# Rows of means loaded ahead of the fourth input tile, norming by single token tiles, and transposes shifted by a group

## The chip, the cores and the metric

One Trainium2 chip, and one of its cores. The metric is the device time of one launch in microseconds (us), the median of several runs of the same program. Engines are named as the profile names them: PE is TensorE (PEld its weight loads), DVE is VectorE, ACT is ScalarE, POOL is GpSimd, and SP is SyncE, whose queue (SPq) issues nearly all DMAs here.

## The reference

The kernel mixes two branches over the same input of 2048 tokens with 576 features, by a gate per token:

```
x = A_x                                           # [1, 2048, 576]
g = _sigmoid((x * gate_w).sum(-1, keepdims=True))
qkv = (x @ wqkv).reshape(B, S, 3, 32, 18)         # 32 heads of 18
p = softmax(q @ k.T * 18 ** -0.5)                 # per head
a = (p @ v).reshape(B, S, D) @ wo
y = layernorm(x)                                  # over the 576 features, no weights
h = gelu(y @ w1 + b1)                             # 4608 wide
b = h @ w2 + b2
out = g * a + (1 - g) * b
```

## The kernel before

All matrix products split an operand into a rounded high part and the rest, and sum three products of such parts. The program has two parts. The first, some 235 us long, projects the input to queries, keys and values and norms it; the second, some 2,000 us, is one long loop that walks 32 units of attention and fills the gaps of PE with the two products of the mixer branch. The change touches the first part alone.

**The first part** runs over four blocks of 512 tokens (`tb` = 0 to 3), each four token tiles of 128. A block has 17 *groups* (`g` = 0 to 16): nine query/key groups (`qk_group`, lines L881 to L884, 14 matmuls of 512 columns, below q0 to q8) and eight value groups (`v_group`, lines L902 to L905, 14 matmuls of 288 columns, v9 to v16; even and odd halves `n` of the four token tiles). In the blocks 2 and 3 the query/key groups come in the order 4, 0, 1, 2, 3, 5 to 8. Each group takes one of the four accumulator banks of the pool `ps_a`; a query/key group's bank is emptied by a copy on ACT (L887) and a subtraction on DVE (L888), the even value groups' by ACT (L909, L911), the odd ones' by a copy on DVE (L913).

Between the groups of block `tb` stands the work for the next block, at group numbers that the tables `N_AT` and `BLOCK` give:

- `load`: `load_x(tb + 2)` issues two DMAs on SP (L733, 1152 KB, and L736, 128 KB) into one of two buffers for the input.
- `stats`: `norm(.., 0)` and `norm(.., 1)`, in two groups in a row, take mean and variance of the next block on DVE (L844, L845, then a short chain from L850 to L860 with a square root on ACT, L851), and leave them in the tile `stp`.
- `rows`: `stat_rows` turns `stp` with one PE transpose (L826), copies it on ACT (L827), and stores it to DRAM (L828, `st_scr`). `wide`: `load_wide` reads these rows back, spread to all 128 partitions (L832, 512 KB, printed as `qa<-st_scr`). These are the rows of means and of reciprocal deviations, "the means" below.
- `x`: from this group on one `x_chunk` a group for five groups: four PE transposes of 128 columns into one bank (L757, written T0 to T4 below), then on DVE a subtraction that needs the means (L772), a copy on ACT (L774; L778 and L779 in the fifth), and a subtraction on DVE (L775; L780 in the fifth); POOL multiplies by the deviations (L782). The five results are what the next block's groups multiply. `lag` groups later `y_parts` splits the normed chunk (L797 on ACT, L798 on POOL), and one group on `y_store` issues two DMAs (L789, L791).
- `gate`: `norm(.., 2)` and `norm(.., 3)` sum the input times the gate weights on DVE (L867), two token tiles each.

The first block is normed in place instead: `N_AT` says at which group of block 0 which stage runs, and there the stages 2 and 3 also norm the token tile (L870). `y_chunk` (groups 12 to 16 of block 0) transposes the normed tiles again (four transposes, written Y0 to Y4; L805 on ACT, L806 on DVE) and stores them.

In block 1 two *rounds* of attention's first step stand behind the groups 9, 11, 13 and 15 (four matmuls L227 in four banks, each emptied by a DVE reduction L229); they need queries and keys that SP has loaded back (L136). A call of `after(n, f)` runs `f` in `next_turn`, right behind the n-th following group.

Every engine and the SP queue take their instructions in the order in which the code writes them, so a group number moves an instruction on its engine and in every queue that it uses. Which bank a tile of `ps_a` gets follows from that order too. The loop of a block, with its hooks:

```
for g, (fn, args) in enumerate(work):
    ...
    fn(*args)
    next_turn()
    ...
    if tb + 1 < NB:
        at = BLOCK[tb]
        if g == at.get("load"):
            load_x(tb + 2)
        ...
        c = g - at["x"]
        if 0 <= c < 5:
            x_chunk(tb + 1, c)
            after(at["lag"], lambda tb=tb, c=c: y_parts(tb + 1, c))
```

Of the kernel before, what the change touches and what calls it, by code (L numbers as in the profile page):

```python
# [54 lines left out]
          lambda g: 2 * (g in (4, 5, 6, 7, 8, 10, 12, 14))]  # L55
SLOTS = [lambda g: 0, lambda g: 0, lambda g: int(g >= 4), lambda g: 1 if g < 9 else 2]
SKIP = 0
N_AT = {3: 0, 4: 1, 7: 2, 8: 3}
BLOCK = [dict(stats=0, rows=3, wide=4, x=10, lag=4, gate=15, load=16),
         dict(stats=6, rows=9, wide=10, x=12, lag=3, gate=8, load=10),  # L60
         dict(stats=0, rows=3, wide=4, x=6, lag=3, gate=4)]
W_AT = {0: 1, 1: 2, 2: 3, 4: 4, 6: 5, 7: 6}
W_CUT = (0, 128, 416, 704, 992, 2 * D, 3 * D - 288, 3 * D)
NSTEP = 512
# [4 lines left out]
def gated_mix_kernel(ctx: ExitStack, tc: tile.TileContext, x, wqkv, wo, w1, b1, w2, b2, gate_w, out):  # L69
    nc = tc.nc  # L70
    x = x[0]
# [20 lines left out]
    gate = const.tile([P, NT], F32, name="gate")  # L92
# [612 lines left out]
    with ExitStack() as a:  # L705
# [9 lines left out]
        stats = wpool.tile([P, NT, 2], F32, name="stats")  # L715
# [3 lines left out]
        wide = QA[2].bitcast(F32).rearrange("p (a n) -> p a n", a=2)  # L719
# [81 lines left out]
        def y_chunk(tb, c):  # L801
            ps = transposed(tb, c)
            eh = hp.tile([P, TB], F32R, name="hh")
            el = hp.tile([P, TB], F32R, name="hl")
            nc.scalar.activation(eh, ps, AF.Copy)  # L805
            nc.vector.tensor_tensor(el, ps, eh.bitcast(F32), op=ALU.subtract)  # L806
            y_store(tb, c, eh, el)
# [4 lines left out]
        def after(n, fn):  # L812
            queued.append((turn[0] + n, fn))
# [9 lines left out]
        def stat_rows(tb):  # L823

            ps = psum(ps_a)
            nc.tensor.transpose(ps[:, :P], stp, ident)  # L826
            nc.scalar.activation(strow, ps[:8, :P], AF.Copy)  # L827
            nc.sync.dma_start(st_scr[tb], strow)  # L828
# [4 lines left out]

        rstds, junks = {}, {}

        def norm(tb, stage):

            xv = x_view(tb)
            ts_ = slice(4 * tb, 4 * tb + 4)
# [21 lines left out]
            if stage >= 2:  # L861
                if stage == 2:
                    junks[tb] = pp.tile([P, 2, 2, TB], F32, name="p").rearrange("p a b c -> p (a b c)")
                junk = junks[tb]
                for t in (2 * stage - 4, 2 * stage - 3):
                    tt = 4 * tb + t
                    nc.vector.scalar_tensor_tensor(junk[:, :D], xv[:, t, 0:D], 1.0, gwb, op0=ALU.mult, op1=ALU.mult,  # L867
                                                   accum_out=glog[:, tt:tt + 1])
                    if tb == 0:
                        nc.vector.tensor_scalar(xv[:, t, :], xv[:, t, :], stats[:, tt, 0:1], rstds[tb][:, t:t + 1],  # L870
                                                op0=ALU.subtract, op1=ALU.mult)
# [66 lines left out]
        for tb in range(NB):  # L938
            work = [(qk_group, (tb, mt)) for mt in (range(9) if tb < 2 else (4, 0, 1, 2, 3, 5, 6, 7, 8))] + [(v_group, (tb, t, n)) for t in range(4) for n in range(2)]
            for g, (fn, args) in enumerate(work):  # L940
# [12 lines left out]
                next_turn()  # L953
                if tb == 0:
                    if g in N_AT:
                        norm(0, N_AT[g])
                    if g >= 12:
                        y_chunk(0, g - 12)
                if tb + 1 < NB:
# [3 lines that stand above are left out]
                    if g in (at["stats"], at["stats"] + 1):  # L963
                        norm(tb + 1, g - at["stats"])
                    if g == at["rows"]:
                        stat_rows(tb + 1)
                    if g == at["wide"]:
                        load_wide(tb + 1)
                    if g in (at["gate"], at["gate"] + 1):
                        norm(tb + 1, g - at["gate"] + 2)  # L970
                    c = g - at["x"]
                    if 0 <= c < 5:
                        x_chunk(tb + 1, c)
                        after(at["lag"], lambda tb=tb, c=c: y_parts(tb + 1, c))
# [344 lines left out]
```

## Time and profile before

| | before |
|---|---|
| median of 3 runs | 2248.53 us (2248.34 to 2248.68) |
| the profiled execution, its own time | 2250.38 us |
| its span in the trace | 2248.6 us |
| PE busy in the span | 2219.2 us, 99% |
| DVE, ACT, POOL busy | 1643.9, 1426.9, 1003.9 us |
| first part, until the loop begins | about 235 us |

The span runs from the first to the last recorded instruction. PE is busy nearly everywhere, so an edit can only gain where PE stands still or runs at a lower clock, and such places are read from PE's waits and from windows with the granted clock. In the rows of the timeline the first number is the start of a row in us from the start of the span, the second its length; several instructions of a line may be merged into one row (`x12`), and square brackets tell how long the engine was idle before it and what released it.

### The profile page before, as it was taken

The page shows a single profiled execution, that of the slowest core. Times are in us where ns is not written, and L with a number is a line of the kernel's source. Part 1 is how long each engine was busy: PE and PEld are TensorE (multiplying, and loading weights), DVE is VectorE, ACT ScalarE, POOL GpSimd, SP SyncE. Part 2 cuts the span into 40 slices and gives each one's busy share as a digit, 9 for nine tenths or more (in the row PEclk, how much of TensorE's full clock was granted, in tenths as well). Part 3 has the DMA queues.
Part 4 walks back from the last instruction along what each step waited for, and adds up shares of the span by engine and source line. Part 5 has one row for each costly group of instructions (what it writes and reads, how often), then busy time and mean ns, then how long its engine had stood idle before and what let it go on. Part 6 is the DMA issues. An engine that isn't in the chain of part 4 may idle for free.

```text
span 2248.6 us, 51575 instructions
## 1 busy us (share of the span) xinstructions
PE 2219.2 (99%) x20528; PEld 1585.2 (70%) x20528; DVE 1643.9 (73%) x2886; ACT 1426.9 (63%) x2653; POOL 1003.9 (45%) x1001
## 2 busy tenths in 40 slices
PE   8999999999999999999999999999999999999998
PEld 7877766767766777666676767767676676677668
DVE  6576677777777777777777777777776777777734
ACT  3223677777766666666666666666666666666771
POOL 3232666666655444444454444444444444444700
PEclk9999999999999999999999999999999999999999
DMA  7847654444456524333354424233364323242264
GB/s 239 274 155 250 205 177 158 145 157 149 135 199 176 152 101 153 109 114 112 116 145 154 143 95 143 97 121 103 117 178 144 107 99 119 104 145 95 87 221 166
DMA packets 164104, 329.23 MB, mean 146 GB/s; under 512 B 56814, under 2 KB 84074, under 8 KB 153134
## 3 DMA queue, kind: packets, MB, share of 16 engines
q1 hardware_dynamic: 161766, 322.19, 44.3%
q8 instruction: 162, 2.65, 0.5%
q10 hardware_dynamic: 1968, 3.70, 0.4%
q14 instruction: 80, 0.66, 0.1%
q0 software_dynamic: 128, 0.03, 0.0%
HBM read 233.47 MB, written 96.17 MB: 147 GB/s over the span
## 4 chain that ended last, share of the span: by engine, by line
PE 90%; DVE 4%; DMA 2%; ACT 2%; issue 1%; POOL 1%; SPq 0%; ACTq 0%; DVEq 0%; POOLq 0%
PE ps L285 20%; PE ps L572 19%; PE ps L484 19%; PE ps L267 13%; PE ps L227 10%; PE ps L881 3%; PE ps L1204 2%; DVE m L229 2%; PE ps L902 1%; DMA x<-in_B_w_dram 1%; ACT zz L537 0%; POOL w L180 0%; DMA qa<-st_scr 0%; DMA p<-in_A_wqkv_dram 0%; DVE p L772 0%
## 5 line engine op out<-in xcount | busy, mean ns | idle before, releaser
L229 DVE TENSOR_REDUCE m<-ps 128x1 f32<-128x512 f32 x2048 | 1312.3, 685 | 408.2 <-PE ps L227 385.6
L270 ACT ACTIVATE p<-ps 128x512 f32<-128x512 f32 x1368 | 741.2, 596 | 380.6 <-PE ps L267 377.0
L484 PE MATMUL ps<-big,w 64*128 64x512 f32 x3708 | 568.6, 393 | 1.0 <-DVE z L504 0.6
L180 POOL TENSOR_SCALAR zz<-zz 128x512 f32<-128x512 f32 x288 | 178.4, 619 | 749.3 <-ACT zz L537 734.5
L270 ACT ACTIVATE ring<-ps 128x512 f32<-128x512 f32 x680 | 369.1, 596 | 190.2 <-PE ps L267 188.2
L572 PE MATMUL ps<-w,hh 64*128 64x288 f32 x4352 | 483.9, 294 | 1.8 <-DVE x L589 0.9
L267 PE MATMUL ps<-qa,ka 56*128 56x512 f32 x2048 | 459.7, 422 | 3.2 <-ACT p L270 1.8
L572 PEld LDWEIGHTS ps<-w,hh 64*128 64x128 f32 x4352 | 424.0, 186 | 30.1 <-DVE x L589 3.3
L227 PE MATMUL ps<-ka,qa 54*128 54x512 f32 x2048 | 435.4, 398 | 0.7
L484 PEld LDWEIGHTS ps<-big,w 64*128 64x128 f32 x3708 | 370.0, 187 | 66.1 <-DVE z L504 1.1
L180 POOL TENSOR_TENSOR zz<-zz,z 128x512 f32<-128x512 f32 x288 | 371.8, 1291 | 24.0
L267 PEld LDWEIGHTS ps<-qa,ka 56*128 56x128 f32 x2048 | 213.6, 184 | 221.0 <-DVE m L229 181.0
L572 PE MATMUL ps<-w,hl 64*128 64x288 f32 x2176 | 348.1, 292 | 0.8 <-POOL hl L180 0.8
L285 PE MATMUL ps<-p,vt 128*32 128x512 f32 x2560 | 322.8, 598 | 0.0
L227 PEld LDWEIGHTS ps<-ka,qa 54*128 54x128 f32 x2048 | 219.4, 185 | 25.7 <-DVE m L229 6.2
L572 PEld LDWEIGHTS ps<-w,hl 64*128 64x128 f32 x2176 | 231.5, 185 | 1.2 <-POOL hl L180 1.1
L180 POOL TENSOR_TENSOR hl<-zz,hh 128x512 fp32r<-128x512 f32 x136 | 176.7, 1299 | 11.4
L180 POOL TENSOR_TENSOR w<-x,w 128x576 fp32r<-128x576 f32 (+1 forms) x54 | 98.8, 1843 | 167.1 <-ACT w L392 151.5
L285 PE MATMUL ps<-ring,vt 128*32 128x512 f32 x1280 | 168.7, 598 | 0.0
L285 PEld LDWEIGHTS ps<-p,vt 128*32 128x32 f32 x2560 | 67.0, 109 | 142.7 <-issue 136.5
L881 PE MATMUL ps<-big,wqk 128*128 128x512 f32 x432 | 110.1, 404 | 0.8 <-DVE wqk L752 0.8
L589 DVE SCALAR_TENSOR_TENSOR x<-ps,x 128x288 f32<-128x288 f32 x256 | 104.1, 448 | 8.6 <-PE ps L572 8.6
(124 smaller groups left out, 1494.2 us busy)
## 6 DMA issues: line engine op xcount, KB each, us to landing
w<-w_scr SPq DMA_DIRECT2D x54, 1152.0 KB
w<-w_scr SPq DMA_DIRECT2D x108, 576.0 KB
x<-in_B_w_dram SPq DMA_DIRECT2D x72, 288.0 KB
w_scr<-w SPq DMA_DIRECT2D x18, 1152.0 KB
w_scr<-w SPq DMA_DIRECT2D x36, 576.0 KB
qa<-qk_scr SPq DMA_DIRECT2D x192, 72.0 KB
ka<-qk_scr SPq DMA_DIRECT2D x84, 144.0 KB
qk_scr<-hh SPq DMA_DIRECT2D x36, 256.0 KB
```

The costliest lines, as they stand in the source:

```text
L180: fn(*args, **kw)
L227: nc.tensor.matmul(ps, qa[r0:r0 + 54, t * P:(t + 1) * P], ka[r0:r0 + 54, kb * TB:(kb + 1) * TB], start=True, stop=True)
L229: nc.vector.tensor_reduce(M4[u][:, h, t, kb:kb + 1], ps, axis=AX.X, op=ALU.max)
L267: nc.tensor.matmul(ps[h], ka[r0:r0 + 56, kc * P:(kc + 1) * P], qa[r0:r0 + 56, qb * TB:(qb + 1) * TB], start=True, stop=True)
L270: nc.scalar.activation(RING[n % 3][:, qb, h], ps[h], AF.Exp, scale=SCALE)
L285: nc.tensor.matmul(OB[u][r:r + 32, :], v[:, k, 19 * h:19 * h + 32], RING[c % 3][:, qb, h, :], start=(k == 0), stop=(k == NT - 1))
L484: nc.tensor.matmul(ps[h], wt[w_][r, c, :], y[r, c, :], start=(k == 0), stop=(k == 26))
L572: mm = nc.tensor.matmul(ps[nn][:, :ND], h_[r, tok], w_[p_][r, cs[nn]], start=(k == 0), stop=(k == 6 * G - 1))
L589: nc.vector.scalar_tensor_tensor(dst, ps[nn][:, :ND], 0.5, b2b[:, cs[nn]] if g == 0 else dst, op0=ALU.mult, op1=ALU.add)
L881: nc.tensor.matmul(ps, w_[:, c, ms], big[:, s_, :], start=(k == 0), stop=False)
L902: nc.tensor.matmul(ps[:, :ND], big[:, s_, tok], w_[:, c, cs], start=(k == 0), stop=False)
L1204: nc.tensor.matmul(ps[:, :ND], OT[b][2][:, s_, tok], w_part(w_, c)[:, cs], start=(k == 0), stop=(k == 13))
```

## The change

Two tables get other numbers, `norm` takes a list of token tiles, and the gate sums go through `after`:

```
-N_AT = {3: 0, 4: 1, 7: 2, 8: 3}
-BLOCK = [dict(stats=0, rows=3, wide=4, x=10, lag=4, gate=15, load=16),
-         dict(stats=6, rows=9, wide=10, x=12, lag=3, gate=8, load=10),
-         dict(stats=0, rows=3, wide=4, x=6, lag=3, gate=4)]
+N_AT = {3: (0, ()), 4: (1, ()), 7: (2, (0,)), 8: (3, (1,)), 9: (3, (2,)), 10: (3, (3,))}
+BLOCK = [dict(stats=0, rows=4, wide=5, x=11, lag=4, gate=16, load=16),
+         dict(stats=5, rows=8, wide=9, x=11, lag=3, gate=7, load=13),
+         dict(stats=0, rows=3, wide=4, x=6, lag=3, gate=3)]
...
-        def norm(tb, stage):
+        def norm(tb, stage, part=None):
...
-                for t in (2 * stage - 4, 2 * stage - 3):
+                for t in part or (2 * stage - 4, 2 * stage - 3):
...
-                        norm(0, N_AT[g])
+                        norm(0, *N_AT[g])
...
-                    if g in (at["gate"], at["gate"] + 1):
-                        norm(tb + 1, g - at["gate"] + 2)
+                    if g == at["gate"]:
+                        for k in range(2):
+                            after(k + 1, lambda tb=tb, k=k: norm(tb + 1, k + 2))
```

No operation is added or taken away. In block 0 the means of block 1 move from group 3 (and 4) to 4 (and 5), its transposes from group 10 to 11, and the gate sums of block 1 from behind the groups 15 and 16 to behind the first two groups of block 1. In block 1 the statistics of block 2, their rows and the load of the means move a group ahead, and so do the transposes (12 to 11), while the fourth input tile is loaded at group 13 instead of 10. In blocks 1 and 2 the gate sums stay in their groups. The second part of the program keeps its order on every engine.

The order of the SP queue at the end of block 1, before (L832 is the load of the means, L733 and L736 that of the fourth input tile, L916 stores a value tile):

```order
L891 DMA qk_scr<-hl 128x512
L828 DMA st_scr<-strow 8x128
L136 DMA ka_107<-qk_scr 18x512 x6
L916 DMA v_scr<-vt_109 128x780
L733 DMA x<-in_A_x_dram 128x4x576
L736 DMA x<-in_A_x_dram 128x4x64
L832 DMA qa_106<-st_scr 128x1024
L916 DMA v_scr<-vt_110 128x780
```

and now:

```order
L891 DMA qk_scr<-hl 128x512
L828 DMA st_scr<-strow 8x128
L832 DMA qa_106<-st_scr 128x1024
L136 DMA ka_107<-qk_scr 18x512 x6
L916 DMA v_scr<-vt_109 128x780
L916 DMA v_scr<-vt_110 128x780
L733 DMA x<-in_A_x_dram 128x4x576
L736 DMA x<-in_A_x_dram 128x4x64
```

The load of the means moved past six key loads, a value store and the input tile, and stands right behind the store of its own rows; the input tile moved behind a second value store.

DVE in block 0 from the seventh query/key group's subtraction on, before (L867 and L870 are gate sum and norming of one token tile, L913 empties the bank of the value group v10, L772 and L775 belong to T0):

```order
L888 TENSOR_TENSOR hl<-ps,hh 128x512
L867 SCALAR_TENSOR_TENSOR p,glog<-x,gwb 128x576
L870 TENSOR_SCALAR x<-x,stats,rstd 128x640
L867 SCALAR_TENSOR_TENSOR p,glog<-x,gwb 128x576
L870 TENSOR_SCALAR x<-x,stats,rstd 128x640
L888 TENSOR_TENSOR hl<-ps,hh 128x512
L867 SCALAR_TENSOR_TENSOR p,glog<-x,gwb 128x576
L870 TENSOR_SCALAR x<-x,stats,rstd 128x640
L867 SCALAR_TENSOR_TENSOR p,glog<-x,gwb 128x576
L870 TENSOR_SCALAR x<-x,stats,rstd 128x640
L913 COPY vt_109<-ps 128x8x2x18
L772 TENSOR_TENSOR p<-ps,qa_106 128x512
```

and now:

```order
L888 TENSOR_TENSOR hl<-ps,hh 128x512
L867 SCALAR_TENSOR_TENSOR p,glog<-x,gwb 128x576
L870 TENSOR_SCALAR x<-x,stats,rstd 128x640
L888 TENSOR_TENSOR hl<-ps,hh 128x512
L867 SCALAR_TENSOR_TENSOR p,glog<-x,gwb 128x576
L870 TENSOR_SCALAR x<-x,stats,rstd 128x640
L867 SCALAR_TENSOR_TENSOR p,glog<-x,gwb 128x576
L870 TENSOR_SCALAR x<-x,stats,rstd 128x640
L913 COPY vt_109<-ps 128x8x2x18
L867 SCALAR_TENSOR_TENSOR p,glog<-x,gwb 128x576
L870 TENSOR_SCALAR x<-x,stats,rstd 128x640
L772 TENSOR_TENSOR p<-ps,qa_106 128x512
```

The four token tiles still stand ahead of L772, but the copy L913 is now ahead of the last of them.

DVE at the end of block 1, before, from the gate sums of block 2 on (L229 are the reductions of a pair of rounds):

```order
L867 SCALAR_TENSOR_TENSOR p,glog<-x,gwb 128x576 x4
L229 TENSOR_REDUCE m_1035<-ps 128x1 x4
L913 COPY vt_109<-ps 128x8x2x18
L229 TENSOR_REDUCE m_1035<-ps 128x1 x4
L913 COPY vt_110<-ps 128x8x2x18
L772 TENSOR_TENSOR p<-ps,qa_106 128x512
L775 TENSOR_TENSOR big<-ps,big 128x512
L772 TENSOR_TENSOR p<-ps,qa_106 128x512
```

and now:

```order
L867 SCALAR_TENSOR_TENSOR p,glog<-x,gwb 128x576 x4
L229 TENSOR_REDUCE m_1036<-ps 128x1 x4
L913 COPY vt_109<-ps 128x8x2x18
L772 TENSOR_TENSOR p<-ps,qa_106 128x512
L775 TENSOR_TENSOR big<-ps,big 128x512
L229 TENSOR_REDUCE m_1036<-ps 128x1 x4
L913 COPY vt_110<-ps 128x8x2x18
L772 TENSOR_TENSOR p<-ps,qa_106 128x512
```

The first chunk of block 2 now stands ahead of the second group of reductions instead of behind it.

## The prediction

> **What bounds the kernel now.** I read the page first: one core, and PE busy in nearly the whole span.
>
> ```profile
> span 2248.6 us, 51575 instructions
> PE 2219.2 (99%) x20528; PEld 1585.2 (70%) x20528; DVE 1643.9 (73%) x2886; ACT 1426.9 (63%) x2653; POOL 1003.9 (45%) x1001
> ```
>
> So DVE, ACT or POOL time saved is worth nothing by itself; only a stretch in which PE stands still, or is clocked down, can give anything. The second view is busy time by window, cut at the program's stages:
>
> ```profile
> 0.00:66.00 66.00, 56.85 (x302) 48.87 (x303) 40.03 (x86) 28.54 (x49) 28.20 (x30) 0.97 0.78 246
> 66.00:100.00 34.00, 34.00 (x160) 27.82 (x159) 18.31 (x46) 7.45 (x16) 4.95 (x4) 1.00 0.89 285
> 100.00:134.00 34.00, 27.15 (x148) 22.26 (x147) 20.51 (x39) 7.22 (x17) 10.14 (x8) 0.90 0.46 157
> 134.00:235.00 101.00, 100.73 (x552) 80.53 (x550) 67.60 (x130) 35.51 (x65) 26.29 (x18) 1.00 0.68 221
> 235.00:2248.60 2013.60, 2000.42 (x19377) 1405.69 (x19373) 1497.46 (x2588) 1348.22 (x2509) 934.31 (x942) 1.00 0.42 137
> ```
>
> The columns are the stretch, its length, busy us of PE, PEld, DVE, ACT and POOL, the granted PE clock, DMA share and GB/s. PE idles and loses clock in two places of the first part: block 0, and the seam of blocks 1 and 2 (100 to 134 us: 6.85 us idle at a mean clock of 0.90). The change works exactly there. Whose fault it is, PE's waits before 235 us say (waiter, releaser, total, times, longest):
>
> ```profile
> PE ps L883 <- DVE big L780: 3.6, 1, 3.6
> PE ps L757 <- ACT v L911: 3.1, 1, 3.1
> PE ps L902 <- DVE vt L913: 2.1, 1, 2.1
> PE ps L826 <- DVE stp L860: 1.2, 1, 1.2
> ```
>
> Each costs more than itself, as finer windows show (same columns; each low window stands behind the stall that precedes it):
>
> ```profile
> 47.10:50.50 3.40, 1.27 (x11) 1.03 (x9) 3.33 (x9) 0.00 (x0) 0.00 (x0) 1.00 0.43 144
> 50.60:53.90 3.30, 3.30 (x15) 3.28 (x15) 1.98 (x4) 1.59 (x4) 2.21 (x2) 0.50 0.46 160
> 115.40:118.80 3.40, 3.40 (x17) 2.98 (x15) 3.29 (x6) 0.08 (x1) 0.81 (x1) 0.50 0.01 2
> 129.10:132.40 3.30, 3.30 (x9) 2.52 (x9) 2.52 (x7) 0.89 (x2) 1.28 (x1) 0.50 0.58 200
> 23.30:26.60 3.30, 2.10 (x10) 1.43 (x10) 2.27 (x11) 3.00 (x6) 1.42 (x1) 1.00 0.62 203
> ```
>
> After the stalls of 2.1, 3.1 and 3.6 us PE ran some 3.4 us at half clock; 1.2 us idle within such a window (the last row) cost no clock. All told the stalls are 10.0 us and the three half-clock windows at most 1.7 us each, so about 15 us are to be had: a floor of 2233 us.
>
> **The seam of blocks 1 and 2, which carries the sum.** These rows tell its story:
>
> ```profile
> 91.64 2.96 PE L881 MATMUL ps<-big,wqk 128*128 128x512 f32 x12
> 94.91 1.76 PE L902 MATMUL ps<-wv,big 128*128 128x288 f32 x12
> 96.56 0.17 DVE L860 COPY stp<-rstd 128x4 f32<-128x4 f32 x1
> 97.77 0.30 SPq L828 DMA_DIRECT2D st_scr<-strow  x1
> 103.59 0.43 SPq L733 DMA_DIRECT2D x<-in_A_x_dram  x1
> 104.71 0.69 SPq L832 DMA_DIRECT2D qa<-st_scr  x1
> 112.21 0.69 DVE L772 TENSOR_TENSOR p<-ps,qa 128x512 f32<-128x512 f32 x1 [6.28 <-DMA qa<-st_scr]
> ```
>
> DVE stood 6.28 us before T0's subtraction, for the means, whose load was issued behind 1280 KB of input tile and landed 7.5 us later. Behind L772 on DVE queue the reductions, the copies and the other chunks; T2 then lacks a bank (3.1 us), and block 2's first group lacks its fifth chunk (3.6 us, L780).
>
> In the changed kernel statistics stand a group earlier, so `stp` is ready before q8 ends (94.91, where v9 starts) instead of at 96.73. L826 follows q8 directly. Before, L828 came 1.04 after `stp`, which from 94.91 would be 95.95; but SP issues q8's own stores first, which wait for DVE's subtraction, so I take 97.0 for L828. From there to L832 the trace has two cases:
>
> ```profile
> 32.68 0.71 SPq L828 DMA_DIRECT2D st_scr<-strow  x1
> 37.60 0.32 SPq L832 DMA_DIRECT2D qa<-st_scr  x1
> 145.44 0.44 SPq L828 DMA_DIRECT2D st_scr<-strow  x1
> 147.90 0.32 SPq L832 DMA_DIRECT2D qa<-st_scr  x1
> 154.33 0.68 DVE L772 TENSOR_TENSOR p<-ps,qa 128x512 f32<-128x512 f32 x1
> ```
>
> L832 waits for the rows' store: it came 2.46 us behind it for the means of block 3 (written in block 2), 4.92 for those of block 1 (written in block 0). Its landing shows nowhere, but in the block-3 case L772 ran 6.43 us later without a wait, which bounds it from above; from below, 512 KB at that seam's 315 GB/s are 1.7 us:
>
> ```profile
> 104.70:112.20 7.50, 6.13 (x46) 5.37 (x44) 1.23 (x3) 0.00 (x0) 0.00 (x0) 1.00 0.99 315
> 101.00:103.00 2.00, 1.90 (x11) 1.12 (x9) 2.00 (x5) 0.50 (x2) 0.00 (x0) 1.00 0.25 69
> ```
>
> So the means land between 97.0 + 2.46 + 1.7 = 101.2 and 97.0 + 4.92 + 6.43 = 108.3. The DMA engines ran nearly empty from 101 on and nothing of size now stands ahead of L832, so I take 104.0, nearer the lower end. DVE cannot start L772 before 102.6 anyway:
>
> ```profile
> 100.33 2.48 DVE L229 TENSOR_REDUCE m<-ps 128x1 f32<-128x512 f32 x4
> 102.72 0.45 DVE L913 COPY vt<-ps 128x288 f32<-128x288 f32 x1
> ```
>
> In the new order L229 x4 and one L913 precede L772, 0.6 us earlier than here.
>
> From L772 to the end of block 2's first group the trace took 128.68 − 112.21 = 16.5 us. The new order holds the same DVE work between L772 and L780 (five chunks, two fours of reductions, two copies), so I keep 16.5: the group ends at 120.5. PE alone would need until about 118.5: T0 stands one value group behind 99.81, from its end near 102 follow five value groups of 1.95 (the step of the first two rows below), four transposes of 0.35, three fours of rounds of 0.7 and a query group of 3.27 (91.64 to 94.91). So DVE still leads there by 2 us, spread over several waits of at most 1.3 us in 3.4: no half clock. The gain is 128.68 − 120.5 = **8.2 us**, and the next group runs at full clock, 4.50 − 2.96 = **1.5 us** more:
>
> ```profile
> 97.86 1.85 PE L902 MATMUL ps<-wv,big 128*128 128x288 f32 x12
> 99.81 1.76 PE L902 MATMUL ps<-wv,big 128*128 128x288 f32 x12
> 128.68 4.50 PE L881 MATMUL ps<-big,wqk 128*128 128x512 f32 x12
> ```
>
> What is late next is DVE itself, which enters block 2 with a full queue: statistics and reductions push the third pair of rounds **0.4 us** out.
>
> [...]
>
> **Block 0.** Two stalls. The 1.2 us ahead of L826 vanish, since q4 now runs first. But q5 needs a weight split of POOL's that the change does not hasten, and v10 needs the last split, whose weights land late:
>
> ```profile
> 41.82 1.66 DVE L752 TENSOR_TENSOR wv<-p,wv 128x1440 fp32r<-128x1440 f32 x1 [5.12 <-ACT wv L751]
> 49.89 0.45 DVE L913 COPY vt<-ps 128x288 f32<-128x288 f32 x1
> 51.60 0.69 DVE L775 TENSOR_TENSOR big<-ps,big 128x512 fp32r<-128x512 f32 x1 [0.66 <-ACT big L774]
> 54.68 1.84 PE L902 MATMUL ps<-wv,big 128*128 128x288 f32 x12
> 65.42 3.05 PE L881 MATMUL ps<-big,wqk 128*128 128x512 f32 x12
> ```
>
> v10 cannot pass 43.2 or so, so 0 to 0.4 us of the first stall survive. The 2.1 us stall was v12 waiting for L913 (49.89). L913 now precedes the fourth token tile, so v12 runs at once. But DVE's total is unchanged: T0's L775 still ends near 52.0, and v13 now takes T0's bank, so PE waits there (about 1.5 us, after 0.7 us in which Y0 waits for the last norming). At 52.0 PE starts v13, which before began at 54.68. From there to block 1's first group the trace took 65.42 − 54.68 = 10.74; one transpose more falls behind it now (0.35), and I add 0.3 for banks that DVE frees late. It starts at 63.4 instead of 65.42: **2.0 us**. Bounds: 0.5 us (splits as late as before, and the leftover 2.2 us fall into one clock window) and 3.2 (no waits after v13).
>
> **Edits at nothing.** Block 1's gate sums (L867 x4, 3.1 us) move under q0 and q1 of block 1, where DVE is busy 18.31 of 34 us; uncovered they would cost their 3.1 us. The `y_store` DMAs of block 1 come a group later; L887's buffers wait for them, and four banks give three groups of cover, 3 × 3.27 us. The fourth input tile is issued near 109 behind a second value store (which waits for L913 on DVE), should land by 116, and is first read near 122. SP, while L832 waits, holds back six key loads for rounds in block 2 and a value store whose buffer is wanted near 110.
>
> **Sum.** 8.2 + 1.5 − 0.4 + 2.0 = 11.3 us. From the seam on every engine keeps its order, so the rest shifts whole. The profiled execution spans 2248.6 us within 2250.38; the median is 2248.53, and I subtract there: **2237.2 us**. With the costs' ends: means at 102.6 and block 0 at 3.2 give 2234.6; means at 108.3, block 0 at 0.5 and one more half-clock window (1.6) give 2244.6.
>
> **Rivals.**
> 1. *The means stay late.* The wait for the rows' store takes the place of the input tile: DMA share is 0.89 before 100 us, and block 0 needed 4.92. Landing at 108.5 to 112 leaves 0 to 4 us at the seam, 2242 to 2246, say 2244. Against it: for block 3's means the same pair took 2.46, and the queue empties after 101. Chance 0.14.
> 2. *Slower, by the key and query loads.* The first rounds (behind v9, so at about 97) wait for twelve loads. With the normed stores a group later, these loads queue behind them; PE is in order, so each us late costs one. It decides from 11 us, with loads landing past 108: 2250 at 113 − 97 = 13 us late. The store volume that moves past is 512 KB, 1.7 us, which speaks against. Chance 0.06.
> 3. *Block 0 only moves its waits.* Its 2.0 become 0 and the seam holds: 2239; it lies inside the forecast.
>
> **Numbers.** Forecast 0.80, rivals 0.14 and 0.06. A run of this kernel tells some 0.2%, 4.5 us, from no change. The forecast lies under 2244.0 almost wholly, rival 1 half: faster 0.86, same 0.08, slower 0.06. The range, 2234.0 to 2245.5, holds the forecast's ends and most of rival 1.
>
> **What would show it.** L832 ahead of L733, L772 idle for under 2 us instead of 6.28, block 2's first group ending some 10 us earlier; no window at 0.50 behind 60 us; in block 0 the wait on L913 replaced by one on L775 before v13. Wrong it would be with a wait of L772 of 5 us or more, a PE wait for `ka<-qk_scr`, or BN statistics of block 3 waiting for the input tile.

## The result and the profile after

| | before | changed |
|---|---|---|
| median of 8 runs each, on one chip | 2248.46 us (2247.76 to 2250.06) | 2241.74 us (2240.36 to 2242.58) |
| ratio of the times, 95% interval | | 0.9968, 0.9958 to 0.9979 |
| the profiled execution, its own time | 2250.38 us | 2240.88 us |
| its span in the trace | 2248.6 us | 2239.1 us |

The kernel became 6.7 us faster by the medians. The forecast was 2237.2, 11.3 us faster, with a range of 2234.0 to 2245.5: direction and range hold, and the gain is a little over half of what was forecast.

The two profiled executions differ by 9.5 us, but 1.2 us of that lies behind the last matmul. These are PE's last rows of the timeline, first of before:

```profile
2243.17 0.30 PE L1204 MATMUL ps<-wlast,big 128*128 128x288 f32 x1
```

and of the changed kernel (its lines there are one higher):

```profile
2234.90 0.30 PE L1205 MATMUL ps<-wlast,big 128*128 128x288 f32 x1
```

The last matmul stands 2243.17 − 2234.90 = 8.27 us earlier. From the issue of the last store (2244.06 before, 2235.78 after) to the end of the span it took 4.5 us before and 3.3 after, for the same store. All of the 8.27 us are there by 134 us. Busy time by stage of the changed kernel (columns as in the prediction):

```profile
0.00:66.00 66.00, 58.18 (x307) 49.39 (x308) 39.38 (x85) 27.92 (x47) 26.96 (x29) 0.97 0.79 246
66.00:100.00 34.00, 34.00 (x165) 27.91 (x164) 22.13 (x51) 8.42 (x18) 5.15 (x4) 1.00 0.88 287
100.00:134.00 34.00, 32.12 (x173) 25.23 (x172) 25.57 (x56) 10.09 (x23) 12.76 (x10) 1.00 0.59 209
```

At the seam of blocks 1 and 2 PE was busy 27.15 of 34 us at a mean clock of 0.90; it is now busy 32.12 at 1.00. Block 0 still has a mean clock of 0.97. The waits of PE before 235 us show what is left (not shown are 0.4 us for a weight split, 0.2 without a named cause, and the 4.8 us that PE waits for the first input tile, as before):

```profile
PE ps L757 <- DVE big L775: 1.4, 1, 1.4
PE ps L902 <- DVE big L775: 1.3, 1, 1.3
PE ps L881 <- POOL wqk L752: 0.7, 1, 0.7
PE ps L757 <- DVE x L870: 0.4, 1, 0.4
```

The stalls of 3.6, 3.1, 2.1 and 1.2 us are gone; in their places stand 1.4 at the seam, and 1.3, 0.7 and 0.4 in block 0. Short waits inside a merged row count mostly as busy and are not in this list. Two such rows stand at the seam, fours of rounds that took 2.23 and 1.94 us, where the two fours ahead of them took 0.73 each; their weight loads waited 2.2 us for DVE's reductions L229:

```profile
107.90 2.23 PE L227 MATMUL ps<-ka,qa 54*128 54x512 f32 x4
114.85 1.94 PE L227 MATMUL ps<-ka,qa 54*128 54x512 f32 x4
```

How the means came, from the timelines of SP and DVE:

```profile
93.16 0.34 SPq L890 DMA_DIRECT2D qk_scr<-hh  x1
95.66 0.60 SPq L891 DMA_DIRECT2D qk_scr<-hl  x1
96.35 0.56 SPq L828 DMA_DIRECT2D st_scr<-strow  x1
101.47 0.32 SPq L832 DMA_DIRECT2D qa<-st_scr  x1
105.15 0.69 DVE L772 TENSOR_TENSOR p<-ps,qa 128x512 f32<-128x512 f32 x1 [3.99 <-DMA qa<-st_scr]
110.41 0.42 SPq L733 DMA_DIRECT2D x<-in_A_x_dram  x1
```

L832 now precedes the input tile (L733), as the change says, yet DVE still waits 3.99 us at L772, since L832 itself came 5.12 us behind L828. PE's rows that mark the progress (block 1's first query/key group, block 2's first two, and the third):

```profile
64.25 2.12 PE L881 MATMUL ps<-big,wqk 128*128 128x512 f32 x8
118.67 2.96 PE L881 MATMUL ps<-big,wqk 128*128 128x512 f32 x12
121.93 2.96 PE L881 MATMUL ps<-big,wqk 128*128 128x512 f32 x12
125.95 3.06 PE L881 MATMUL ps<-big,wqk 128*128 128x512 f32 x12
```

Block 1 starts 1.17 us earlier than before (65.42), block 2's first group ends 6.75 us earlier (121.93 against 128.68), and the third group starts 8.29 us earlier (125.95 against 134.24); at the last matmul the difference is 8.27.

### The profile page after: what moved, and what is told of

It reads as the page before. It is cut to its first block, busy times and chain, and to the rows that moved or that the text cites. A ratio compares the mean times of both kernels' runs of the same rounds, so it can differ in the third digit from the quotient of the medians.

```text
span 2239.1 us, 51576 instructions
## 1 busy us (share of the span) xinstructions
PE 2216.3 (99%) x20528; PEld 1578.7 (71%) x20528; DVE 1644.1 (73%) x2886; ACT 1427.3 (64%) x2653; POOL 1002.9 (45%) x1001
## 4 chain that ended last, share of the span: by engine, by line
PE 91%; DVE 3%; DMA 2%; ACT 1%; issue 1%; POOL 1%; SPq 0%; DVEq 0%; ACTq 0%; POOLq 0%
PE ps L285 20%; PE ps L572 20%; PE ps L484 20%; PE ps L267 13%; PE ps L227 11%; PE ps L881 3%; PE ps L1205 2%; DVE m L229 1%; PE ps L902 1%; DMA qk_scr<-hl 1%; ACT zz L537 0%; DMA x<-in_B_w_dram 0%; PE ps L757 0%; DMA p<-in_A_wqkv_dram 0%; DVE hl L888 0%
## 5 line engine op out<-in xcount | busy, mean ns | idle before, releaser
L229 DVE TENSOR_REDUCE m<-ps 128x1 f32<-128x512 f32 x2048 | 1311.3, 683 | 408.8 <-PE ps L227 384.2
```

What stands on the lines that cost most here:

```text
L229: nc.vector.tensor_reduce(M4[u][:, h, t, kb:kb + 1], ps, axis=AX.X, op=ALU.max)
```

## The experiments

Five marks are read from each kernel's profile: the start of block 1's first group, the start of DVE's first L772 in block 2's chunks and its wait, the end of block 2's first group (the start of its second), the start of its third group, and the last matmul. From the third group on all kernels run the same order; still, what lies between it and the last matmul differs by up to 2.4 us from profile to profile (2106.98 to 2109.41). The times before in the four comparisons were 2248.46, 2248.67, 2248.98 and 2249.09; the ratio is to the runs of before in the same comparison.

| kernel | block 1 starts | L772 (wait) | block 2: first group ends | third group starts | last matmul | median | ratio, 95% interval |
|---|---|---|---|---|---|---|---|
| before | 65.42 | 112.21 (6.28) | 128.68 | 134.24 | 2243.17 | 2248.5 | |
| changed | 64.25 | 105.15 (3.99) | 121.93 | 125.95 | 2234.90 | 2241.74 | 0.9968, 0.9958 to 0.9979 |
| changed, again | 63.65 | 104.90 (4.35) | 123.49 | 127.51 | 2235.28 | 2240.04 | 0.9959, 0.9946 to 0.9971 |
| seam only | 65.83 | 105.05 (2.31) | 121.86 | 125.88 | 2233.34 | 2239.76 | 0.9963, 0.9950 to 0.9975 |
| seam only, again | 64.97 | 103.58 (1.73) | 120.36 | 124.39 | 2232.76 | 2240.55 | 0.9965, 0.9952 to 0.9977 |
| block 0 only | 63.66 | 110.40 (6.19) | 127.32 | 133.66 | 2241.18 | 2247.22 | 0.9993, 0.9984 to 1.0002 |
| load only | 65.56 | 107.88 (1.82) | 124.80 | 129.83 | 2237.80 | 2245.64 | 0.9984, 0.9975 to 0.9993 |
| input tile ahead again | 63.97 | 111.22 (10.36) | 129.10 | 133.12 | 2240.92 | 2246.01 | 0.9990, 0.9981 to 0.9999 |
| early means | 65.40 | 102.57 (0.15) | 119.35 | 123.37 | 2230.35 | 2235.71 | 0.9941, 0.9929 to 0.9954 |
| early means, old block 0 | 65.90 | 102.82 (none) | 119.60 | 123.62 | 2232.61 | 2237.74 | 0.9950, 0.9937 to 0.9964 |
| early means, early norming | 62.40 | 99.87 (0.46) | 116.67 | 120.69 | 2228.94 | 2234.93 | 0.9936, 0.9923 to 0.9948 |
| early means, old transposes | 63.88 | 103.66 (none) | 120.75 | 126.00 | 2235.12 | 2239.84 | 0.9957, 0.9943 to 0.9971 |
| early means, norming in pairs | 64.11 | 102.07 (0.95) | 118.87 | 122.89 | 2232.30 | 2237.28 | 0.9948, 0.9936 to 0.9961 |
| both early, transposes earlier | 62.10 | 99.44 (2.40) | 118.20 | 122.22 | 2230.62 | 2237.39 | 0.9951, 0.9938 to 0.9963 |

### The change taken apart

**Seam only**: the kernel before with the numbers of block 1.

```
-         dict(stats=6, rows=9, wide=10, x=12, lag=3, gate=8, load=10),
+         dict(stats=5, rows=8, wide=9, x=11, lag=3, gate=8, load=13),
```

> Only the numbers of block 1 are changed (statistics at 5, rows 8, means 9, transposes 11, fourth input tile 13); block 0 stays as before. The last matmul of the changed kernel stands 8.3 us earlier than that of the kernel before (2234.90 against 2243.17). Theory A, the seam carries the gain and block 0 adds about 1.2 us by itself: the last matmul stands 7.1 us earlier than before, L772's wait for the means is some 4 us instead of 6.28, half-clock windows at 115 and 129 us are gone, median 2241 to 2243. Rival B, the two edits need each other (the seam gains only because block 0 hands over earlier): under 4 us earlier, median above 2244.5.

**Block 0 only**: the changed kernel with block 1's old numbers.

```
-         dict(stats=5, rows=8, wide=9, x=11, lag=3, gate=7, load=13),
+         dict(stats=6, rows=9, wide=10, x=12, lag=3, gate=7, load=10),
```

> Only block 0 is changed (norming by single token tiles, the transposes of block 1 at 11, its means at 5, its gate sums under block 1); block 1's numbers are those of before. Theory A: block 1's first query/key group starts 1.2 us earlier than before (64.25 against 65.42), the stall of 6.3 us at the means and the two half-clock windows of the seam stay, the last matmul stands 1.2 us earlier, median 2247 to 2248. Rival B (what block 0 gives is lost again at the seam, since the input tile sets the arrival of the means): 0 to 0.3 us earlier at the last matmul.

At block 2's third group the seam alone is worth 134.24 − 125.88 = 8.4 us, more than the 7.1 of theory A and as much as the whole change (8.3); the median of 2239.76 is below the range that was expected. Its last matmul stands 9.8 us earlier, against 8.3; 0.9 us of this last difference is a longer wait on ACT just ahead of the end, of the seam-only kernel first, then of the changed one:

```profile
2218.36 1.57 PE L1204 MATMUL ps<-big 128*128 128x288 f32 x10 [0.34 <-ACT big L1128]
```

```profile
2219.93 1.57 PE L1205 MATMUL ps<-big 128*128 128x288 f32 x10 [1.28 <-ACT big L1129]
```

Block 0 alone gives 0.6 us at the third group, 2.0 at the last matmul and 1.5 in the median, with an interval of the ratio that just reaches 1. The parts do not add up: the seam alone is worth the whole. SP and DVE of the seam-only kernel say why:

```profile
97.33 0.31 SPq L828 DMA_DIRECT2D st_scr<-strow  x1
101.15 0.32 SPq L832 DMA_DIRECT2D qa<-st_scr  x1
105.05 0.69 DVE L772 TENSOR_TENSOR p<-ps,qa 128x512 f32<-128x512 f32 x1 [2.31 <-DMA qa<-st_scr]
```

Here block 1 began 1.58 us later than in the changed kernel (65.83 against 64.25), and still the means came at the same time, 105.05 against 105.15. DVE only waits less for them, 2.31 instead of 3.99. PE shows the same: the two slow fours at the seam took 2.19 and 1.95 us here, as in the changed kernel, but the stall of 1.43 us on L775 ahead of them, which took up the changed kernel's earlier start, is not among this kernel's waits.

**Load only**: one number, `load=10` becomes `load=13` in block 1. On SP the means' load then precedes the input tile, and no other engine's order changes.

> The kernel before with one number changed: the fourth input tile is loaded at group 13 of block 1 instead of 10, so that the load of the means stands ahead of it; no other instruction moves on any engine. Theory A, the input tile ahead of the means made the seam: the means are loaded near 103.5 (behind one value store), arrive near 107.2 instead of 112.2, the last matmul stands 6 to 6.5 us earlier, median 2242 to 2243. Rival C, the shift of the statistics and the transposes by a group carries it: under 2 us earlier, median above 2246.

```profile
103.72 0.43 SPq L832 DMA_DIRECT2D qa<-st_scr  x1
107.88 0.69 DVE L772 TENSOR_TENSOR p<-ps,qa 128x512 f32<-128x512 f32 x1 [1.82 <-PE ps L905]
123.78 0.80 PE L883 MATMUL ps<-big,wqk 128*128 128x512 f32 x1 [3.67 <-DVE big L780]
```

The third group starts 4.4 us earlier, the last matmul stands 5.4 earlier, and the median fell by 3.0: between the two theories. L772 moved 4.3 us, but the transposes stand a group later than in the changed kernel, so PE still reaches the fifth chunk 3.67 us too soon and loses clock behind it (the next row of twelve matmuls took 3.98 us, 2.96 in the changed kernel). The input tile was the larger part of the old stall, not all of it. (The row puts the wait of L772 down to a matmul of a value group that T0 does not use. L772 started 4.16 us behind L832, near the 3.68 and 3.90 of the two kernels whose rows name the means, so the means probably released it, but this row does not settle it.)

**Input tile ahead again**: the changed kernel with `wide=10, load=10` in place of `wide=9, load=13`.

> The changed kernel with two numbers of block 1 put back: the means are loaded at group 10, and the fourth input tile at group 10 ahead of them. Theory A: the means arrive near 111 again, DVE waits about 10 us at L772 (the transposes stand a group earlier than before, so the wait begins earlier), the last matmul stands 7 to 8 us later than in the changed kernel (near 2242 to 2243), median 2248 to 2250. Rival C (the shift carries it): the last matmul at most 3 us later, median under 2245.

```profile
111.22 0.69 DVE L772 TENSOR_TENSOR p<-ps,qa 128x512 f32<-128x512 f32 x1 [10.36 <-DMA qa<-st_scr]
```

As theory A said at L772, and block 2's first and third groups stand 7.2 us later than in the changed kernel. At the last matmul 6.0 are left, and the median of 2246.01 is 2 us below the range that was expected. Rival C, that the shift carries the gain, falls for this kernel.

### What sets the arrival of the means

**Changed, again** and **seam only, again**: both without an edit, in one comparison with the next two.

> The changed kernel once more, beside the seam-only kernel on one chip. In their traces both stand level at the seam (block 2's second group at 121.93 and 121.86) though block 1 begins 1.6 us earlier in the changed kernel, so block 0's gain is lost in the wait for the means. Theory D, the means' arrival is set by DMA engines that are full until 100 us, not by PE: the medians of the two kernels differ by less than 1 us here. Rival E, the single-tile norming costs something later in the program: the changed kernel stays 1.5 to 2.5 us slower (2241.7 against 2239.8 so far).

> The seam-only kernel once more, beside the changed kernel. Theory D: within 1 us of the changed kernel's median. Rival E: 1.5 to 2.5 us faster than it.

Side by side their medians are 0.5 us apart, 2240.04 and 2240.55, with ranges that overlap (2237.95 to 2241.26, 2238.75 to 2243.81), as theory D expected. The 2 us that parted them in two comparisons did not come back. (Their profiles are 3.1 us apart at the third group. Of this 1.3 stand already at L772, since the means came later in the changed kernel though its block 1 began earlier; why is open. The rest comes behind it: the changed kernel's ran 6.8 us at half clock at the seam, the other's none; the last section comes back to it.)

Theory D says that full DMA engines pace the means. DMA share in the changed kernel (the column before the last; it sums the times of packets, so it can pass 1), from 94 us:

```profile
94.00:96.00 2.00, 2.00 (x17) 1.84 (x17) 1.36 (x3) 0.82 (x3) 0.00 (x0) 1.00 1.07 347
96.00:98.00 2.00, 2.00 (x15) 1.63 (x14) 1.91 (x5) 0.42 (x2) 0.00 (x0) 1.00 1.11 284
98.00:100.00 2.00, 2.00 (x17) 2.00 (x16) 2.00 (x5) 0.00 (x0) 0.00 (x0) 1.00 0.62 166
100.00:102.00 2.00, 2.00 (x16) 1.47 (x15) 1.16 (x3) 0.50 (x2) 0.00 (x0) 1.00 0.00 0
```

and the DMAs that it issued from 93 to 97 us:

```profile
qk_scr<-hh SPq DMA_DIRECT2D x3, 256.0 KB
qk_scr<-hl SPq DMA_DIRECT2D x3, 256.0 KB
...
st_scr<-strow SPq DMA_DIRECT2D x1, 4.0 KB
```

SP had been busy with key and query loads from 86.46 to 93.06 us; then it issued the stores of q6, q7 and q8 from 93.16 to 96.26, 1.5 MB, and the 4 KB of the rows behind them. The engines were full until about 99 us (share 1.07 and 1.11, then 0.62 from 98 to 100), and L832, which waits for those 4 KB, could go at 101.47. The last 2 us of its wait passed with the engines empty (0.00 in the last window), so the stores ahead are not the whole of the 5.12 us. Nor is it a fixed time behind the rows' store: in the seam-only kernel, where the same three pairs stand ahead and L828 itself came 0.9 to 1.0 us later, it took 3.82 us, and 3.36 in the second profile.

**Early means**: the changed kernel with the rows ahead of the stores of q7 and q8.

```
-         dict(stats=5, rows=8, wide=9, x=11, lag=3, gate=7, load=13),
+         dict(stats=2, rows=6, wide=7, x=11, lag=3, gate=7, load=13),
```

> The changed kernel with the statistics of block 2 at group 2, their rows at 6 and the load of the means at 7, so that the 4 KB store of the rows no longer stands behind the stores of q7 and q8 on the DMA engines. Theory D (the rows' store waits behind 1.5 MB of stores that SP issues between 93 and 97 us): the load of the means is issued near 97 instead of 101.5, the means arrive near 100.5 instead of 105.1, L772 waits under 0.5 us instead of 3.99, and the first group of block 2 ends near 118.5 instead of 121.9; the last matmul stands 3 to 4 us earlier, median near 2238. Rival F (a store to DRAM and a load behind it take some 9 us whatever stands ahead of them): the means arrive near 103 and the gain is under 2 us, median above 2239.5.

```profile
94.67 0.38 SPq L891 DMA_DIRECT2D qk_scr<-hl  x1
95.14 0.29 SPq L828 DMA_DIRECT2D st_scr<-strow  x1
95.52 0.32 SPq L890 DMA_DIRECT2D qk_scr<-hh  x1
95.93 0.41 SPq L891 DMA_DIRECT2D qk_scr<-hl  x1
97.93 0.32 SPq L832 DMA_DIRECT2D qa<-st_scr  x1
...
116.09 2.96 PE L881 MATMUL ps<-big,wqk 128*128 128x512 f32 x12
```

With one pair of stores ahead of the rows instead of three, L832 follows L828 by 2.79 us instead of 5.12; the wait at L772 is 0.15 us. The median falls to 2235.71, 4.3 us below the changed kernel in the same comparison. Rival F, a fixed latency of some 9 us, falls: L772 starts 7.43 us behind L828, 8.80 in the changed kernel.

**Early means, old block 0**: as above, with the norming and the numbers of block 0 as before the change.

> As the run before, but with block 0 as it was before the change. With the wait for the means gone, theory D says that block 0's gain now comes through: this kernel stands 1.2 to 2 us behind the other, with its first group of block 2 ending near 120 against 118.5, median near 2239.5. Rival E (block 0's edit costs later): level with the other or ahead of it.

Its median is 2.0 us higher, 2237.74 against 2235.71, and the ranges (2236.90 to 2238.61, 2234.70 to 2236.34) do not meet: with the wait for the means gone, block 0 counts in the median. The two profiles do not show where. They are 0.5 us apart at the start of block 1 (the profiled execution of the early means was granted a clock of 0.50 from 53.5 to 56.8 us, that of the old block 0 1.00 from 47 to 54) and 0.25 at block 2's third group; 2.0 of the 2.26 us at the last matmul come behind it, where profiles differ by as much anyway.

### What block 0 and the transposes are worth

Three kernels vary the early means by one part each, and one by two parts.

**Early norming**: in block 0 all four token tiles are normed at groups 5 and 6, where DVE otherwise stands still for weights (5.50 us ahead of L752 in the changed kernel); the sums' products go to another dead tile.

```
-N_AT = {3: (0, ()), 4: (1, ()), 7: (2, (0,)), 8: (3, (1,)), 9: (3, (2,)), 10: (3, (3,))}
+N_AT = {3: (0, ()), 4: (1, ()), 5: (2, (0, 1)), 6: (3, (2, 3))}
...
-                    junks[tb] = pp.tile([P, 2, 2, TB], F32, name="p").rearrange("p a b c -> p (a b c)")
+                    junks[tb] = b2b if tb == 0 else pp.tile([P, 2, 2, TB], F32, name="p").rearrange("p a b c -> p (a b c)")
```

> The early-means kernel (statistics of block 2 at 2, rows 6, means 7), with the four token tiles of block 0 normed at groups 5 and 6, ahead of the weight split for which DVE stands still 6 us (36.3 to 42.2 us), and with their gate sums written to another dead tile. Theory G, the waits in block 0 come from DVE's order (norming ahead of the transposes' subtractions): T0's L775 ends near 50 instead of 52.7, the waits of v13 and of Y0 (1.5 and 0.4 us) go, no half-clock window stands in block 0, block 1's first group starts near 62 to 63.5 instead of 65.4; the median is 1.5 to 3 us lower than the early-means kernel's (2235.7). Rival H, DMA engines full until 100 us set the pace of block 1 whatever block 0 does: block 1 starts earlier, but the means then make DVE wait 1 to 2 us again at L772, and the median is less than 1 us lower.

The waits on norming and on L775 fall to 0.3 us, a new one of 0.9 appears on ACT, the granted clock is 1.00 from 49 to 66 us, and block 1 starts at 62.40:

```profile
49.15 0.69 DVE L775 TENSOR_TENSOR big<-ps,big 128x512 fp32r<-128x512 f32 x1 [0.67 <-ACT big L774]
54.08 1.84 PE L902 MATMUL ps<-wv,big 128*128 128x288 f32 x12 [0.93 <-ACT v L911]
99.87 0.69 DVE L772 TENSOR_TENSOR p<-ps,qa 128x512 f32<-128x512 f32 x1 [0.46 <-DMA qa<-st_scr]
```

So theory G is right about block 0, L775 ending at 49.8 instead of 52.7. Block 2's first and third groups stand 2.7 us earlier than with the early means alone, the last matmul 1.4, and the median only 0.8, in another comparison, with ranges that overlap (2233.37 to 2235.64). That is the size of rival H, but not its mechanism, since DVE waits 0.46 us, not 1 to 2. Part of the 2.7 belongs to one execution, since the profile of the early means holds a half-clock window in block 0 and was the slowest of its five runs (2236.34). What takes the rest between 123 us and the end is open. It is the kernel with the lowest median of the study.

**Old transposes**: the transposes of block 2 from group 12 again (`x=12`).

> The early-means kernel with the transposes of block 2 back at group 12. In all runs so far the first group of block 2 ends 16.5 to 16.9 us behind the start of DVE's first L772. Theory A, the shift of the transposes is worth what it moves L772: with the second four reductions and a copy ahead of it, L772 starts near 105.8 instead of 102.6 although the means are there, the first group of block 2 ends near 122.6 instead of 119.35, median 3 us or more above 2235.7. Rival I, once the means are early the transposes' place is indifferent: within 1 us of 2235.7.

```profile
103.66 0.69 DVE L772 TENSOR_TENSOR p<-ps,qa 128x512 f32<-128x512 f32 x1
119.86 0.67 PE L883 MATMUL ps<-big,wqk 128*128 128x512 f32 x1 [2.60 <-DVE big L780]
```

The median is 4.1 us higher, 2239.84. L772 has nothing to wait for but stands behind a second four of reductions; block 1 began 1.52 us earlier here, and still L772 is 1.09 us later, so the shift is worth 2.6 us at L772; PE stalls for 2.6 us again, and half clock follows (the next row of twelve matmuls took 4.19 us instead of 2.96). Theory A; its number of 105.8 was for a block 1 that starts at 65.4.

**Norming in pairs**: `N_AT` with pairs at groups 7 and 8 as before the change, on the early means.

> The early-means kernel with the norming of block 0 in pairs at groups 7 and 8 again (the transposes of block 1 stay at 11, their means at 5). Theory J, splitting the norming is what block 0 gains by: the copy L913 stands behind all four token tiles again, PE waits some 2 us for a bank, and block 1's first group starts as in the kernel with the old block 0 (65.9 against 65.4 in one execution each, half-clock windows apart), median near 2237.7. Rival K, the shift of the means' rows and of the transposes gains it: as the early-means kernel, 2235.7.

Not settled. The median, 2237.28, is where theory J put it, but block 1 starts at 64.11, against 63.65 to 63.97 in four profiles with the split norming and this block 0 (the other two, at 64.25 and 65.40, had a half-clock window there): 0.1 to 0.5 us, not 1.5. The medians of the two kernels come from two comparisons, and the changed kernel itself moved by 1.7 us between two.

**Both early, transposes earlier**: the early norming with `x=10, gate=4`.

> The early norming of block 0 together with the gate sums of block 2 at groups 5 and 6 instead of 8 and 9, and the transposes of block 2 at 10. Theory G: PE in the early-means kernel works 20.1 of the 21.1 us from v9 to block 2's first group, so at most 0.9 us more is to be had at the seam: the median is 0 to 0.9 us under that of the early norming alone. Rival H: the means' arrival sets it, no difference, or DVE waits at L772 for 2 to 4 us without cost to PE.

A miss for both theories: 2237.39, 2.5 us above the early norming alone. DVE waits 2.40 us at L772; two chunks now stand ahead of the second reductions, and the rounds that need their banks take longer:

```profile
104.55 1.85 PE L227 MATMUL ps<-ka,qa 54*128 54x512 f32 x4
110.77 2.29 PE L227 MATMUL ps<-ka,qa 54*128 54x512 f32 x4
```

Undisturbed such a four takes 0.73 us, and in the early norming alone these two took 0.73 and 1.67. Block 2's first and third groups stand 1.5 us later than with the early norming alone, though block 1 started 0.3 us earlier.

## Why the prediction was right, and where not

**What bounds the kernel** was read rightly: the gain came from PE's stalls and lost clock ahead of 134 us and stood complete there, though by the parts taken alone it came from the seam. The 10.0 us of stalls left out 4.8 at the kernel's start, which the change does not touch, and 1.3 of smaller ones.

**From L828 to the means: mis-sized.** L828 came at 96.35; on the clock of before, on which block 1 starts 1.17 later, that is 97.5 against the 97.0 of the prediction. For the wait behind it the prediction had 2.46 and 4.92 us from two other blocks, and took the means' landing at 104.0, "nearer the lower end", since the DMA engines ran nearly empty from 101 us (share 0.25). But the rows' store is issued at 97, when they are full (share 1.11 from 96 to 98 us in the changed kernel); the prediction left that to its first rival. The wait was 5.12, above both bounds, and the load took at most 3.68 us more (to the start of L772). The early means, with one pair of stores ahead instead of three, took 2.33 us off the wait behind L828.

**From L772 to the end of block 2's first group** the prediction kept 16.5 us. It took 16.78 in the changed kernel, and 16.5 to 16.9 in ten of the fourteen profiles, with L772 starting anywhere from 99.87 to 112.21. The other four have 17.1 to 18.8: the one whose chunks start at group 10, and three in which PE ran at half clock ahead of that end. Half clock alone does not set these apart, since before, block 0 only and load only had half clock there too (the first row of L883 behind the stall of L780 took 0.79 us in block 0 only and 0.80 in load only, 0.40 at full clock; before had 0.50 at 115.4 us). What paces the stretch is DVE: the five L772 start 4.72, 1.95, 4.71 and 1.95 us apart in the changed kernel, and within 0.01 us the same in its second profile, where PE ran 6.8 us of it at half clock. So the start of L772 is the lever of this seam, with two limits. In the early means PE's rows leave no gap behind it, from 102.57 to 119.35 us (short waits included), so there the stretch is about as long for PE. And with both early, where the chunks stand in another order, L772 starts 0.4 us earlier than with the early norming alone, but the group ends 1.5 later. The seam alone gave 128.68 − 121.86 = 6.8 us, or 7.2 counted from the start of block 1 (65.83 against 65.42), where the prediction had 8.2.

**The clock at the seam** gave what was forecast: 8.29 − 6.75 = 1.54 us against 1.5. But it is not so in every execution (below).

**The full queue of DVE**, −0.4, did not show: from block 2's second group to its third, with a pair of rounds between, it took 125.95 − 121.93 = 4.02 us, and the group's 3.27 and the rounds' 0.7 are 3.97 of them.

**Block 0 by itself** was right in its steps: L913's stall gone, PE waiting for the last norming (0.40 us, 0.7 forecast) and then for T0's L775 (1.27, 1.5 forecast):

```profile
49.89 0.77 PE L757 MATMUL ps<-ident,x 128*128 128x128 f32 x5 [0.40 <-DVE x L870]
51.93 2.48 PE L902 MATMUL ps<-wv,big 128*128 128x288 f32 x12 [1.27 <-DVE big L775]
52.80:56.20 3.40, 3.40 (x18) 3.38 (x17) 1.23 (x2) 1.53 (x4) 1.28 (x1) 0.51 0.69 259
```

v13 started at 51.93, 52.0 in the prediction. Block 1 started at 64.25 instead of 63.4 because PE ran the next 3.4 us at half clock (the third row), the case that the prediction named as its lower end; in the changed kernel's second profile, without that window, it started at 63.65, though v13 came later there, at 52.58.

**The step that failed is the sum.** "8.2 + 1.5 − 0.4 + 2.0" adds block 0's gain to the seam's, which holds only while the means' arrival moves with PE. Before the change it did: the input tile was issued behind a value store that waits for DVE (L913 on DVE ended at 103.17, its store went at 103.20, the tile's load L733 at 103.59), and in the block-0-only kernel L772 came 1.8 us earlier (110.40), the first group's end 1.4. In the changed kernel block 1 started 1.3 to 1.6 us earlier than with the old block 0 (64.25 and 63.65 against 65.83 and 64.97), but L832, which in both waits for the rows' store with three pairs of stores ahead of it, came no earlier (101.47 and 100.69 against 101.15 and 99.85): DVE waited 3.99 and 4.35 us at L772 instead of 2.31 and 1.73, and the end did not come earlier. The seam-only kernel shows the sum without block 0: 6.8 us at the first group's end and 1.5 by the clock, 8.4 in all; the changed kernel has 6.75 and 1.54. The 2.0 of block 0 added nothing, and the 8.2 of the seam came to some 7. On the changed kernel's own clock the sum has the means at 104.0 − 2.0 = 102.0 and the first group's end at 120.5 − 2.0 = 118.5. L772 started at 105.15, 3.15 us later, and the group ended at 121.93, 3.4 later; less the 0.4 that did not show, that is the 3.0 us between the forecast gain of 11.3 and the profiles' 8.3.

**Between the 8.3 us of the profiles and the 6.7 of the medians**: the second comparison gave 2248.98 − 2240.04 = 8.9, and both intervals hold 8.3. Executions of the changed kernel differ in their half-clock windows: the profiled one had a single one, in block 0, its second profile two, at the seam.

**Edits at nothing.** They cost nothing: PE was busy in all of the stretch from 66 to 100 us while DVE's busy time there rose from 18.31 to 22.13 us; the fourth input tile was issued at 110.41 (109 forecast), and block 3's statistics did not wait for it. **The rivals.** The first, means late by the rows' store, is the mechanism of the 3 us that were lost, at a smaller price than its 108.5 us. The second did not occur: PE never waited for `ka<-qk_scr`. The third, block 0 moving its waits, ended as it said, nothing of block 0 at the end, but for another reason. Of the signs, the wait of L772 came out between the two marks (3.99 us, with under 2 forecast and 5 or more named as wrong), and block 2's first group ended 6.75 us earlier instead of some 10.

## What to carry to other kernels

Before adding the gains of two places, ask what paces the transfer that the later place waits for: the load issued behind a value store that waits for DVE came earlier with that work here (L772 by 1.8 us in the block-0-only kernel), the one issued behind a 4 KB store with 1.5 MB of stores ahead of it did not (105.15 against 105.05 us, with block 1 1.58 us earlier), and a gain ahead of it only became waiting. Try a small store that a load waits for ahead of the large ones: here 4 KB stored two groups earlier (with its statistics three groups earlier) gave 4.3 us on top of the change's 8.9 in the same comparison. And where one wait is removed, look for the next instruction whose start the later work follows at a fixed distance (here DVE's first subtraction, 16.5 to 16.9 us ahead of the end of the next block's first group in ten of the fourteen profiles), and ask first what moves that.

## What the runs showed of the hardware

**Half clock came in windows of 3.41 us, and not in every execution.** Between 11 us and the last matmul, the kernel before was granted 0.50 in three single windows of 3.41 us, which start at 50.54, 115.39 and 129.04 us, 19 and 4 windows apart, and the changed kernel in one, at 52.84. The changed kernel's second profile had two in a row, 109.28 to 116.10, at 0.50. Against the start of the kernel the windows lie differently in each execution: counted in 3.41 us from 50.54, neither 52.84 nor 51.70 (in the seam-only kernel) falls on one. Rows of this length show the stretch ahead of the half clock in block 0 of the changed kernel, then the stretch that holds the seam's stall of 1.4 us, and the one of the seam-only kernel's second profile that holds most of its 2.15 us stall in block 0:

```profile
49.43:52.84 3.41, 1.74 (x13) 1.47 (x13) 2.75 (x6) 1.09 (x2) 1.27 (x1) 1.00 1.00 265
104.04:107.45 3.41, 1.98 (x16) 1.77 (x15) 1.64 (x3) 0.60 (x1) 1.26 (x1) 1.00 0.50 192
```

```profile
46.63:50.04 3.41, 1.61 (x13) 1.37 (x12) 3.34 (x9) 0.00 (x0) 0.00 (x0) 1.00 0.38 123
```

and, from the changed kernel's second profile, the window with most of the seam's stall of 1.8 us and the one behind it:

```profile
105.87:109.28 3.41, 2.04 (x7) 0.97 (x7) 3.03 (x6) 0.35 (x1) 1.07 (x1) 1.00 0.00 0
109.28:112.70 3.42, 3.31 (x13) 2.88 (x13) 2.30 (x5) 1.42 (x4) 1.66 (x2) 0.50 0.60 160
```

The windows with PE busy 1.74 and 2.04 us were followed by half clock, those with 1.98 and 1.61 were not. So the busy time of these rows does not decide: it holds short waits inside merged rows (in the 2.04, most of a four of rounds that took 2.53 us instead of 0.73). What decides is open. The same kernel differs from execution to execution: the seam-only kernel ran a half-clock window at 51.7 us in its first profile and none in its second (1.00 from 46.6 to 54.4 us), behind about the same stall (2.2 and 2.15 us), and the changed kernel had none at the seam in the first and two in a row in the second.

At 1.7 us each at most (half of 3.41), one such window more or less is of the order of the spread of the changed kernel's runs (2.2 us).

**The waiter of a 4 KB store came 2.8 to 5.1 us behind it when large stores had been issued just ahead.** It came 5.12 and 5.06 us behind the store's issue in the two profiles of the changed kernel, with 1.5 MB issued in the 3.2 us ahead of it, 3.82 and 3.36 in those of the seam-only kernel, with 1.5 MB in 3.6 us, and 2.79 in the early means, with one pair, 512 KB, issued in the 0.9 us ahead. What held it for the last 2 us in the changed kernel, at a DMA share of 0.02 and less, is open.
